# A second channel product in 7x7 block products, its inner weight sums in DRAM, and both channel products in one interleaved stream

## The chip, the cores and the metric

One Trainium2 chip, one core. The time is the device time of one execution in microseconds (us), taken over three to six executions of each kernel; the kernel before is run on the same chip in the same rounds. The profile is one execution under the hardware profiler. Its engines: PE is TensorE's matmuls, PEld its weight loads, DVE is VectorE, ACT ScalarE, POOL GpSimd, SPq the queue in which SyncE issues transfers. SBUF and PSUM are the core's two on-chip memories; the tiles of this program whose names begin with ps_ lie in PSUM, its other tiles in SBUF.

## The reference, cut to what matters

```python
kv  = einsum('bhsd,bhse->bhde', k, v)           # B = 8, H = 8, S = 576, D = 64
out = einsum('bhsd,bhde->bhse', q, kv)
x   = out / sqrt(mean(out**2) + 1e-6) * g_norm  # reshaped to (B, S, 512)
h   = maximum(x.T @ w_tok1, 0) @ w_tok2         # token mixing, 576 -> 256 -> 576
u   = x + h.T
h2  = maximum(u @ w_ch1, 0) @ w_ch2             # channel mixing, 512 -> 1536 -> 512
return u + h2                                   # all in fp32
```

The last two products, the "channel products", take two thirds of the time. They are worked on in nine groups of 512 rows. Group 0 is a special case that runs while weights are still being mixed; the eight groups after it are alike and are called steady groups here.

## The kernel before

A matrix product cut into 2x2 blocks needs eight block products, or seven with extra sums of blocks (Strassen's scheme in Winograd's form). Done at two levels it is 7 x 7 = 49 for 64. The first channel product already works so in the steady groups; the second is done at one level. They follow each other.

```python
SA = {1: 0, 2: 1, 7: 2, 4: 3, 5: 4, 6: 5, 3: 6}      # where a block or a sum of blocks lies
def a_of(o, n):                                       # weight block: outer product o, inner product n
    o, n = SA[o], SA[n]
    if o > 3:
        return late["w2"][:, o - 4, n]
    return w_ch1[:, o, n] if n < 4 else late["w1"][:, o, n - 4]   # all in SBUF
...
def channel1(g):                                      # first product: 7 outer x 7 inner
    padd = lambda o, a, b: tensor_add(o, a, b, engine=nc.gpsimd)   # whole 128x1536 sums on GpSimd
    ...
        def product(n, name, start, stop):            # one block product: 3 matmuls of 128 columns
            for w in range(W):
                matmul(at[name][:, w], lhsT=a_of(o, n)[:, ts(w, P)],
                       rhs=uT[g][:, SB[o], SB[n]], start=(start and w == 0), ...)
    ...
def channel2(g):                                      # second product: 7 products, one level
    def product(n, ps, start, stop):                  # 12 matmuls of 256 columns
        for p in range(2):
            for s in range(NS):
                matmul(ps[:, p], lhsT=V[g][n - 1][:, s, p], rhs=w2_of(n)[:, s], ...)
    ...
for g in range(NG):
    fetch_u(g + 1)
    extra = prepare(g + 1, t_psum)                    # transposes and sums for the next group
    ...
    for step in channel1(g):
        step()
    for n, step in enumerate(channel2(g)):
        step()
        for f in extra[n:n + 1]:
            f()
```

## Time and profile before

| | before |
|---|---|
| time, median of 3 runs | 912.71 us (912.62 to 914.88) |
| span of the profiled run, granted TensorE clock | 909.4 us, 0.976 |
| one steady group | 71.10 us |
| TensorE, VectorE, GpSimd busy in it | 71.09, 40.67, 20.67 us |

### The profile page before, as it was taken

How to read it: one execution, taken by the hardware profiler on the slowest of the kernel's cores; microseconds unless marked ns; L12 is line 12 of the kernel's file. 1: busy time of each engine (PE TensorE's matmuls, PEld its weight loads, DVE VectorE, ACT ScalarE, POOL GpSimd, SP SyncE). 2: the span in 40 equal slices, each digit the busy share in tenths (PEclk: the TensorE clock that was granted, in tenths of full speed). 3: DMA queues.
4: the chain of work that ended last, by engine and by line, in shares of the span. 5: the costliest groups of instructions: out<-in, count | busy, mean ns of one | idle time of the engine just before them, and what ended most of it. 6: DMA issues, size and time to landing. Idle time of an engine off the chain costs nothing.

```text
span 909.4 us, 12630 instructions
## 1 busy us (share of the span) xinstructions
PE 858.0 (94%) x5136; PEld 727.7 (80%) x5136; DVE 561.9 (62%) x928; ACT 245.1 (27%) x588; POOL 168.2 (18%) x62
## 2 busy tenths in 40 slices
PE   5479897997999999999999999999999999999997
PEld 5356454563468889889989989989989989989986
DVE  1677887897765695655646736636636546546552
ACT  2556645655311102302301301311211210310210
POOL 1000000000000006304404503602701700800710
PEclk9789998998999999999999999999999999999999
DMA  9994675833140011002001002002002002001002
GB/s 297 325 316 140 242 236 194 264 110 116 39 146 1 1 47 47 1 29 66 1 24 70 1 1 93 1 1 93 1 1 93 1 1 94 1 1 47 1 1 47
DMA packets 43578, 72.54 MB, mean 80 GB/s; under 512 B 2688, under 2 KB 21120, under 8 KB 43520
## 3 DMA queue, kind: packets, MB, share of 16 engines
q1 hardware_dynamic: 42160, 70.53, 23.6%
q10 hardware_dynamic: 1360, 1.21, 0.4%
q8 instruction: 40, 0.66, 0.3%
q14 instruction: 18, 0.15, 0.1%
HBM read 52.85 MB, written 18.87 MB: 79 GB/s over the span
## 4 chain that ended last, share of the span: by engine, by line
PE 82%; DVE 8%; DMA 4%; ACT 3%; issue 1%; POOL 0%; POOLq 0%; SPq 0%; ACTq 0%; DVEq 0%
PE ps_w L127 34%; PE ps_v L127 32%; PE ps_h L127 5%; PE ps_u L127 5%; DMA v_in<-in_v_dram 2%; ACT x L318 2%; PE ps_ut L411 2%; PE ps_kv L127 2%; PE ps_o L127 1%; DVE x L296 1%; DMA raw<-in_moe_w_tok_dram 1%; DVE part L178 1%; ACT sq L295 1%; PE ps_r L127 1%; DVE uT L118 1%
## 5 line engine op out<-in xcount | busy, mean ns | idle before, releaser
L127 PE MATMUL ps_v<-uT,w 128*128 128x128 f32 (+1 forms) x1656 | 209.6, 280 | 0.1
L127 PEld LDWEIGHTS ps_v<-uT,w 128*128 128x128 f32 x1656 | 198.2, 192 | 2.1 <-DVE uT L118 0.3
L118 POOL TENSOR_TENSOR vs<-vs,v 128x1536 f32<-128x1536 f32 x8 | 27.6, 3445 | 668.3 <-DVE vs L118 668.3
L127 PE MATMUL ps_v<-uT,w_ch 128*128 128x128 f32 (+1 forms) x864 | 124.1, 287 | 0.5 <-DVE u L118 0.5
L127 PEld LDWEIGHTS ps_v<-uT,w_ch 128*128 128x128 f32 x864 | 112.3, 192 | 4.6 <-issue 0.8
L127 PE MATMUL ps_w<-d,vs 128*128 128x256 f32 x432 | 96.8, 380 | 0.5 <-DVE vs L118 0.4
L127 PE MATMUL ps_w<-w_ch,v 128*128 128x256 f32 x432 | 96.2, 379 | 0.0
L127 PE MATMUL ps_w<-w_ch,vs 128*128 128x256 f32 x432 | 96.2, 379 | 0.0
L118 DVE TENSOR_TENSOR vs<-ps_v,u 128x384 f32<-128x384 f32 (+1 forms) x123 | 69.0, 561 | 39.7 <-PE ps_v L127 30.9
L127 PEld LDWEIGHTS ps_w<-d,vs 128*128 128x128 f32 x432 | 80.7, 190 | 12.6 <-issue 1.5
L127 PEld LDWEIGHTS ps_w<-w_ch,vs 128*128 128x128 f32 x432 | 81.5, 190 | 10.7
L127 PEld LDWEIGHTS ps_w<-w_ch,v 128*128 128x128 f32 x432 | 80.8, 190 | 10.3
L124 ACT COPY t<-ps_v 128x384 f32<-128x384 f32 (+1 forms) x59 | 28.5, 484 | 210.3 <-PE ps_v L127 193.5
L318 ACT ACTIVATE x<-x,inv 128x64 f32<-128x64 f32 x288 | 70.9, 337 | 16.9 <-DVE inv L314 16.9
L127 PE MATMUL ps_h<-x,w_tok 128*128 128x512 f32 (+1 forms) x160 | 69.2, 625 | 4.0 <-DVE w_tok L118 4.0
L127 PE MATMUL ps_u<-h,w_tok 128*128 128x512 f32 (+1 forms) x160 | 69.2, 623 | 0.0
L118 DVE TENSOR_TENSOR u<-ps_v,t 128x384 f32<-128x384 f32 (+1 forms) x59 | 33.3, 564 | 48.2 <-PE ps_v L127 46.3
L121 ACT ACTIVATE v<-v 128x1536 f32<-128x1536 f32 (+1 forms) x30 | 39.5, 1316 | 72.6 <-DVE v L118 72.6
L118 POOL TENSOR_TENSOR v<-v,vs 128x1536 f32<-128x1536 f32 x16 | 55.1, 3442 | 19.9 <-DVE vs L118 9.7
L118 DVE TENSOR_TENSOR uT<-uT 128x512 f32<-128x512 f32 (+1 forms) x68 | 56.6, 874 | 2.1 <-ACT uT L124 1.6
L118 DVE TENSOR_TENSOR u<-ps_w,u 128x512 f32<-128x512 f32 x18 | 12.4, 692 | 71.2 <-PE ps_w L127 71.2
L127 PEld LDWEIGHTS ps_h<-x,w_tok 128*128 128x128 f32 (+1 forms) x160 | 27.5, 200 | 35.7 <-issue 33.8
(74 smaller groups left out, 926.3 us busy)
## 6 DMA issues: line engine op xcount, KB each, us to landing
qT<-in_q_dram SPq DMA_DIRECT2D x8, 1152.0 KB, 7.7
xg<-u_dram SPq DMA_DIRECT2D x9, 1024.0 KB, 5.6
k_in<-in_k_dram SPq DMA_DIRECT2D x16, 512.0 KB, 5.6
u_dram<-x SPq DMA_DIRECT2D x16, 512.0 KB, 3.0
out_dram<-xg SPq DMA_DIRECT2D x16, 512.0 KB, 2.8
v_in<-in_v_dram SPq DMA_DIRECT2D x14, 512.0 KB, 6.6
raw<-in_moe_w_ch_dram SPq DMA_DIRECT2D x16, 384.0 KB, 5.7
raw<-in_moe_w_ch_dram SPq DMA_DIRECT2D x12, 512.0 KB, 4.0
```

Of the source, the lines that this page charges most:

```text
L118: keep(engine.tensor_tensor(out=o, in0=a, in1=b, op=op))
L121: keep(nc.scalar.activation(o, a, AF.Relu))
L124: keep(nc.scalar.copy(o, a))
L127: keep(nc.tensor.matmul(*a, **kw))
L178: keep(nc.vector.scalar_tensor_tensor(out=part, in0=lo, scalar=2.0 ** -52, in1=part, op0=ALU.mult, op1=ALU.mult))
L295: keep(nc.scalar.activation(sq, o, AF.Square))
L296: keep(nc.vector.tensor_mul(x3, o, g_sb.to_broadcast([P, n * H, D])))
L318: keep(nc.scalar.activation(x3[:, i], x3[:, i], AF.Copy, scale=inv[:, i]))
L411: keep(nc.tensor.transpose(pt[:, c], xg[g][:, i, ts(c, P)], ident))
```

## The change

Its intent is to do the second product at two levels too. That asks for inner sums of both its operands. Those of the weights (for both products now) are no longer kept in SBUF: they are worked out once, written to DRAM in pieces of 576 KB, and one piece is loaded for each outer product, 14 a group. The two products become one stream: one block product is a "place" of 0.67 us, outer product n starts at place 7n, its seven block products are spread over the places 0, 1, 3, 4, 6, 9 and 12 from there, and so they mix with those of the next outer product. Other engines' work is attached to places by `put`. `b` is the first place of a group's second product. The core of the diff, with comments added:

```diff
+    IN = {1: {5: 0, 6: 1, 3: 2}, 2: {5: 0, 6: 1, 4: 2}}
+    def part(weight, o, n, sums=None):
+        if n in IN[weight]:                      # an inner sum: from the loaded piece
+            t = sums[:, IN[weight][n]]
+            return t if weight == 1 else t.rearrange("p (w e) -> p w e", w=W)
 ...
+    PLACE = {1: 0, 2: 1, 6: 3, 5: 4, 7: 6, 4: 9, 3: 12}
+    def outer(place, size, mul, to, base=None):
+        at(1, "a", True, False, lambda: read(temp("t1", 1), 0, 0))   # bank a is read after
+        at(2, "c", True, True)                                       # each of 1, 6, 7, 4
 ...
+    def fetch_sums(n):
+        if n < len(order):
+            w, _, o = order[n]
+            sums[n] = sums_tile()
+            dma(sums[n], sums_dram[w, o])
 ...
+        put(b + 22, *padd(3, 3, 1))              # in channel1: b is the first product's own
+        put(b + 29, *padd(2, 2, 1))              # first place; GpSimd, two halves each
+        put(b + 36, *padd(1, 4, 3))
+        put(b + 43, *padd(7, 5, 4))
 ...
+        put(b - 8, *ins[1][0], ins[1][1])        # in channel2: inner sums of the left operand,
+        put(b + 1, *halves(make_a21))            # "sv", 4 per outer product, on VectorE
+        put(b + 4, *ins[4][0])
+        put(b + 6, *halves(sum1))
+        put(b + 9, ins[4][1], *halves(sum2))
 ...
+        put(b + 63, xadd(0, 1, 3), do(store, g, xg, 0), do(fetch_x, g + 1))
 ...
-    late["xg"] = pool("xg", 2)
+    late["xg"] = pool("xg", 1)
 ...
+    weave(body, lasts + [f for _, f in inner1] + [f for fs, _ in inner2 for f in fs])
+    fetch_x(1)                                   # the passage from group 0 to the stream
+    for n in range(3):
+        fetch_sums(n)
 ...
-        for step in channel1(g):
-            step()
-        for n, step in enumerate(channel2(g)):
-            step()
+    for place in range(max(beside) + 1):
+        if place in products:
+            products[place]()
+        for step in beside[place]:
+            step()
```

## The prediction

> **What bounds the kernel now.** I read the busy shares first, then the chain that ended last, then the instructions in order of time in one steady group, and last what the SyncEngine's DMA queue waited for.
>
> ```profile
> PE 858.0 (94%) x5136; PEld 727.7 (80%) x5136; DVE 561.9 (62%) x928; ACT 245.1 (27%) x588; POOL 168.2 (18%) x62
> PE 82%; DVE 8%; DMA 4%; ACT 3%; issue 1%; POOL 0%; POOLq 0%; SPq 0%; ACTq 0%; DVEq 0%
> PE ps_w L127 34%; PE ps_v L127 32%; PE ps_h L127 5%; PE ps_u L127 5%; DMA v_in<-in_v_dram 2%; ACT x L318 2%; PE ps_ut L411 2%; PE ps_kv L127 2%; PE ps_o L127 1%; DVE x L296 1%; DMA raw<-in_moe_w_tok_dram 1%; DVE part L178 1%; ACT sq L295 1%; PE ps_r L127 1%; DVE uT L118 1%
> ```
>
> TensorE is busy 94% of the span, and two thirds of the chain is the two channel products: ps_v (the first, already seven block products at two levels, 7x7) and ps_w (the second, at one level). By stage (the table of windows) one steady group, 478.2 to 549.3 us, takes 71.10 us, TensorE busy in 71.09 of them and VectorE in 40.67. There are eight such groups; group 0, with weights mixed at one level, is a separate 75 us stage ahead of them. In the chain of waits a steady group reads:
>
> ```profile
> 407.29 32.83 PE ps_v L127 x294
> 440.11 5.18 PE ps_w L127 x24
> 445.30 0.45 PE ps_ut L411 x4
> 445.75 5.40 PE ps_w L127 x24
> 451.59 5.18 PE ps_w L127 x24
> 457.20 5.18 PE ps_w L127 x24
> 462.82 15.54 PE ps_w L127 x72
> ```
>
> The first product is 32.83 us for 294 records (147 matmuls, two records each: fp32). One block product is 6 records, 0.670 us, so 0.1117 us a record of 128 columns. One second-channel product is 24 records of 256 columns, 5.18 us, 0.2159 us a record. A group is 32.83 + 7 x 5.18 + 4 transposes of 0.43 = 70.8 us: nothing else is on the path.
>
> **What the skill says.** "TensorE: Matmul & The Clock Gate", Back-to-back issue gap, gives an isolated gap of N/2.4 + 2.5 ns, 55.8 ns for 128 columns and about 109 for 256. Two passes' worth would be 111.7 and 218; the trace has 111.7 and 215.9. The fixed part is small, so halving the width costs only 3.4% (2 x 111.7 against 215.9). The same page, Why this matters for your kernels, says that a PE gap over about 3 us sends the clock back to half rate; no steady stretch of this trace has such a gap, so it neither confirms nor refutes that. "VectorE: DVE Perf Modes", The perf-mode tier table, has fp32 tensor_tensor at one element a cycle: 128x512 sums take 0.69 us here and 128x1536 1.75, slope 1.04 ns an element, which agrees. "PSUM — Partial Sum Buffer", Engine vs sequencer instructions, has the queues of the three other engines strictly first in, first out: a sum ahead of a bank's read delays that read. The trace shows VectorE serving them in issue order.
>
> **The change, part by part.**
>
> 1. Second product at two levels. Removed per group: 7 x 5.18 = 36.26 us of TensorE. Added: 49 block products of 3 matmuls, 128x128 by 128 columns, the form of the first product: 49 x 0.670 = 32.83. Saved 3.43 us a group. The 0.27 us a group lost to waits (71.1 against 70.83) may go too. Over eight groups **27 to 29 us on the path**. Two levels do 49/56 of the one-level work (-12.5%), of which the narrower matmuls give back three points.
>
> 2. VectorE work per group. Back to back, independent sums start 0.47 us apart at 384 columns, 0.61 at 512, 0.87 at 768 (each duration less some 0.09); a dependent one some 0.12 later. After: first product 8 reads (where a base is added) and 21 writes of 384: 29 x 0.47 = 13.6. u sums, 4 each of 512, 640 and 256: 2.4 + 2.9 + 1.3. Second product: 21 bank reads of 128 columns, about 0.2 each (estimate from the 0.28 of the 128-column kvp copies), 4.2; inner sums of its left operand, new, 28 of 384, 13.2 and some 1.7 for dependence; a21 and sums s1 to s4 in halves, 10 x 0.87 = 8.7; results into x, 11 x 0.61 = 6.7. Sum **55 us**, against 40.7 before, beside 67.4 of TensorE. Overall VectorE fits (81%), but unevenly: from eight places ahead of the second product to its 38th place, 46 x 0.67 + 1.7 of transposes = 32.5 us of TensorE time, I count 14.8 inner sums, 9.0 halves, 3.6 into x, 4.6 and 4.5 bank reads = 36.5. It overflows by 4 us. A write out of bank b has 4 places (2.7 us) before the next product into that bank; a VectorE read of bank a has 2 (1.3 us). So most of the backlog is swallowed and some reaches TensorE. Walking that stretch place by place by hand I find three waits of 0.8, 0.5 and 1.2 us. I take half that, 1.2 us a group, because my sums err to both sides and the placing looks tuned: **+10 us** over eight groups (0 to 20).
>
> 3. ACT and POOL. ACT gets 20 copies of 0.48, 28 of about 0.26, 12 relus of about 0.5 and 4 turns of 0.58: 26 us a group. POOL does 8 halves for 6 wholes of 3.45: about 14 us for 20.7. Both stay far off the path.
>
> 4. Sums in DRAM. 14 pieces of 3x384 floats on 128 partitions are 590 KB each; every block product loads one, 8.3 MB a group, with x (1.05 MB), the transposition source (1.05) and stores (1.05) 11.4 MB in 67 us, 170 GB/s. The early slices carry 297 to 325 GB/s at 94 to 99% busy, so this is half the DMA. A piece is asked for some 11 places (7.4 us) before its first use; 1 MB lands in 5.6 us, so it is hidden, though where x is fetched just ahead of it on the same queue only barely.
>
> 5. Group 0 and the passage to the stream. In the first product of group 0, VectorE takes 21 more sums (9.9 us) into 16.5 us of idle time; in its second, 28 weight sums replace 28. I expect under 1 us there. The passage is another matter: before, VectorE ends it late, and the queue then waits for the store:
>
> ```profile
> 337.40 0.69 DVE L118 TENSOR_TENSOR xg<-ps_w,xg 128x512 f32<-128x512 f32 x1
> ...
> 331.98 6.52 SPq L115 DMA_DIRECT2D out_dram<-xg  x2
> 341.03 0.37 SPq L115 DMA_DIRECT2D xg<-u_dram  x1
> ```
>
> The last ps_w ends at 334.6, the sum into x at 338.1, and the fetch into the freed buffer is issued at 341.03, landing 6 us later. That fetch was not needed for a whole group, so it cost nothing. After, there is one x buffer, and the first pieces of inner sums are asked for *behind* the fetch of x on the same queue. The stream can do two block products (1.3 us) before the third needs a piece. So: 3.5 us to the sum, 2.9 to the store's end, 0.4 issue, then 1.6 MB at 325 GB/s, 5 us, and some 2 of latency: about 13.5 us from TensorE's last product, of which 1.3 is worked through. **12 us of idle TensorE**, and about 1.5 more (estimate from the skill's half clock) until the clock is back, less 1.4 that this passage (72.5 against 71.1) loses today: **+12 us, once**.
>
> 6. The end. The last block products have nothing interleaved between them, so each waits for its bank; final sums and store are as now: +2 us.
>
> Sum: 912.7 - 29 + 10 + 12 - 1 (waits that may overlap) + 2 = 906.7. As the schedule seems laid out with care I shade the VectorE waits to about 6 us: **903 us**.
>
> **Rivals.**
>
> (a) TensorE stays the only bound, passage hidden: 912.7 - 29 + 2 = 886. For: VectorE at 81%, DMA at half, eleven places of lead. Against: the queue order of the passage, which the trace shows waiting for that very store.
>
> (b) VectorE becomes the bound in the second product: its 36.5 us for 32.5 become waits of 4 us a group and 32 in all, 927. For: strict order and dependent sums. Against: the loose places after the 38th and the bank slack.
>
> (c) DMA binds: pieces land late every time x is fetched, 1 us a group or more, +8 to +16. For: store, wait, 1 MB and piece share one queue; it waited 2.5 us for a store seven times already. Against: half the bandwidth is free.
>
> (d) Narrow matmuls are not as quick in the second product as in the first: at 0.125 us a record nothing would be saved. Against: same form, same type, and 0.1117 holds for hundreds of records on end.
>
> **Range and chances.** The gain is firm at 27 to 29 us. Over 2% (under 894.5) leaves only 9 to 11 us for passage, waits and end together; the passage alone eats that unless I misread it: 0.2. Slower by over 2% (over 931) needs (b) and (c) in full: 0.05. Within 2%: 0.75. For 8 in 10: passage 7 to 15, waits 0 to 16, end 0 to 4 give roughly 891 to 917.
>
> **What would show it.** Step 1: second product in 6-record pieces of 0.67 us, ps_w's TensorE time about 32.8 us a group. Step 2: waits of PE for VectorE in the first 35 places of a second product, VectorE busy about 55 us a group or somewhat more. Step 4: no PE wait for DMA in steady groups, some 170 GB/s. Step 5: a PE gap of 8 to 15 us after group 0, ended by the DMA of sums, with the clock below full after it. Wrong if the period of a steady group is over 70 us (waits) or the passage is under 5 us (the queue does not block as I read it).

## More of the kernel before

The page cuts the span into 40 equal slices of 22.7 us; a digit is the busy share in tenths.

```profile
PE   5479897997999999999999999999999999999997
POOL 1000000000000006304404503602701700800710
PEclk9789998998999999999999999999999999999999
```

The steady groups begin in the fifteenth slice. From there TensorE is at 9 in all slices but the last, and its clock in all: next to nothing in these groups keeps it waiting. GpSimd comes in bursts, one per group. What VectorE does during a burst turned out to matter; the instructions in order of time around one burst, GpSimd first, then VectorE (start, duration, engine, line, output and inputs; in brackets the idle time before it and what ended that):

```profile
417.40 3.44 POOL L118 TENSOR_TENSOR vs<-vs,v 128x1536 f32<-128x1536 f32 x1 [46.49 <-DVE vs L118]
435.02 6.98 POOL L118 TENSOR_TENSOR vs<-vs,vs 128x1536 f32<-128x1536 f32 x2
```

```profile
418.77 0.56 DVE L118 TENSOR_TENSOR u<-ps_v,u 128x384 f32<-128x384 f32 x1
442.04 1.76 DVE L454 SCALAR_TENSOR_TENSOR vs<-vs,v 128x1536 f32<-128x1536 f32 x1 [1.33 <-POOL vs L118]
```

During the burst VectorE runs only sums with one operand in PSUM (ps_v), and they take the 0.56 us that they take elsewhere. Its first sum of two SBUF tiles starts at 442.04, after GpSimd's last sum has ended at 442.00, on whose result it waits. The same holds for every other GpSimd sum of this trace: this kernel never has a VectorE sum of two SBUF operands beside one. I did not see that when I predicted.

## The result, and the profile after

The changed kernel took **980.17 us** (978.59 to 981.5, four runs), the kernel before beside it 912.66. The ratio is 1.073 (95%: 1.071 to 1.076): 7% slower, where I had predicted 1% faster. A ratio here and below is the mean time of one kernel's fast runs over that of the other's in the same rounds, so not quite the ratio of the medians. The result is correct.

The page after:

```profile
PE 861.8 (88%) x6144; PEld 761.1 (78%) x6144; DVE 724.5 (74%) x1384; ACT 331.1 (34%) x924; POOL 122.1 (12%) x78
PE   6478997979999868998998999899899799899896
PEclk9789898989999978999999899899899899999998
```

TensorE's row has a 6 in the fifteenth slice (342.9 to 367.3 us), just behind the stream's first products at 336.6, and dips to 8 or 7 again and again after it; the clock's row dips too. In the page's account of the chain that ended last, VectorE has 28%, where it had 8%.

One steady group before and one after, from the table of windows (start:end and length, then busy time and instructions of PE, PEld, DVE, ACT, POOL, then granted clock, DMA share, GB/s):

```profile
478.20:549.30 71.10, 71.09 (x480) 66.34 (x479) 40.67 (x57) 13.66 (x22) 20.67 (x6) 1.00 0.08 30
```

```profile
457.90:534.20 76.30, 70.35 (x606) 69.33 (x606) 59.33 (x112) 24.45 (x64) 14.95 (x9) 0.98 0.45 151
```

This group takes 76.3 us, the mean over the seven periods from 380.64 to 923.02 us is 77.5. Unhindered it would be 98 products of 0.67 and four transposes of 0.43, 67.4 us. So each steady group is 6.4 us longer than before where it should have been 3.7 shorter.

What TensorE waited for from 336 us on (engine and bank, then what it waited for; us in all, times, longest):

```profile
PE ps_a L127 <- DVE t L118: 30.0, 8, 3.8
PE ps_a L127 <- DMA sums<-sums: 17.8, 6, 14.0
PE ps_a L127 <- DVE uT L118: 7.0, 7, 1.0
PE ps_b L127 <- DVE r L118: 6.9, 8, 1.1
PE ps_a L127 <- DVE v L118: 2.6, 9, 1.1
```

(t and u are what is read out of bank a, r and v results of a second and of a first product and sums of them, uT the transposed left operand of the first product with its sums.) Two entries stand out: one wait of some 3.75 us in each of the eight groups, and one of 14.0 us, once. The same view of the kernel before, from 330 us on, has 0.9 us in all.

**The wait of each group.** VectorE in order of time ahead of it, then GpSimd, then TensorE:

```profile
457.07 0.77 DVE L118 TENSOR_TENSOR sv<-v 128x384 f32<-128x384 f32 x1
457.87 2.05 DVE L118 TENSOR_TENSOR sv<-sv,v 128x384 f32<-128x384 f32 x1
459.95 2.04 DVE L118 TENSOR_TENSOR sv<-v,sv 128x384 f32<-128x384 f32 x1
461.92 0.55 DVE L118 TENSOR_TENSOR sv<-v 128x384 f32<-128x384 f32 x1
462.38 0.54 DVE L118 TENSOR_TENSOR t<-ps_a,v 128x384 f32<-128x384 f32 x1
...
471.83 0.56 DVE L118 TENSOR_TENSOR sv<-sv,v 128x384 f32<-128x384 f32 x1
```

```profile
453.82 7.75 POOL L118 TENSOR_TENSOR v<-v,v 128x768 f32<-128x768 f32 x4 [2.74 <-ACT t L124]
```

```profile
458.40 0.83 PE L127 MATMUL ps_a<-uT,w 128*128 128x128 f32 x6
462.98 1.65 PE L127 MATMUL ps_a<-uT,sums 128*128 128x128 f32 x6 [3.75 <-DVE t L118]
464.43 2.26 PE L127 MATMUL ps_b<-uT,sums 128*128 128x128 f32 x12
466.52 0.83 PE L127 MATMUL ps_a<-uT,w_ch 128*128 128x128 f32 x6
```

The product that ended at 459.2 filled bank a. VectorE has to read it (t<-ps_a) before the next product into bank a, but four sv sums were issued ahead of that read. The second and third took 2.05 and 2.04 us, while such a sum some 14 us later, with GpSimd at rest, takes 0.56. GpSimd's four sums run from 453.82 to 461.57, and the first sv sum after that is back at 0.55. The read came at 462.38 and TensorE went on at 462.98. Then it ran at half speed for most of 3.5 us: one product shown with 1.65 us in place of 0.83, two with 2.26 in place of 1.50 (the last product of a row is shown with its modelled end; in a row they start 0.67 apart).

**The passage**, once, from the instructions in order of time (SPq lines are the issue of transfers):

```profile
339.68 0.68 DVE L118 TENSOR_TENSOR xg<-ps_w,xg 128x512 f32<-128x512 f32 x1
340.38 0.39 SPq L115 DMA_DIRECT2D out_dram<-xg  x1
343.63 0.37 SPq L115 DMA_DIRECT2D xg<-u_dram  x1
344.09 3.60 SPq L115 DMA_DIRECT2D sums<-sums  x3
352.12 1.62 PE L127 MATMUL ps_a<-uT,sums 128*128 128x128 f32 x6 [13.98 <-DMA sums<-sums]
```

This is the order of step 5 of the prediction: the sum into x, the store, the fetch of x that waits for the store, and behind it the pieces that TensorE needs. What each link costs, e3 and e7 show below.

### The profile page after: what moved, and what is told of

Same layout as the page of the kernel before. It is cut to its first block, busy times and chain, and to the rows that moved or that the text cites. A ratio compares the mean times of both kernels' runs of the same rounds, so it can differ in the third digit from the quotient of the medians.

```text
span 979.6 us, 16051 instructions
## 1 busy us (share of the span) xinstructions
PE 861.8 (88%) x6144; PEld 761.1 (78%) x6144; DVE 724.5 (74%) x1384; ACT 331.1 (34%) x924; POOL 122.1 (12%) x78
## 4 chain that ended last, share of the span: by engine, by line
PE 53%; DVE 28%; DMA 9%; issue 4%; ACT 4%; SPq 0%; DVEq 0%; ACTq 0%
PE ps_a L127 19%; PE ps_b L127 10%; DVE v L118 7%; DVE sv L118 7%; PE ps_u L127 5%; PE ps_h L127 5%; PE ps_c L127 4%; DMA sums<-sums 4%; PE ps_v L127 4%; PE ps_w L127 3%; ACT x L351 2%; DVE xg L118 2%; DVE uT L118 2%; DVE r L118 2%; DMA out_dram<-xg 2%
## 5 line engine op out<-in xcount | busy, mean ns | idle before, releaser
L118 POOL TENSOR_TENSOR v<-v,v 128x768 f32<-128x768 f32 x64 | 119.4, 1892 | 803.9 <-DVE v L118 779.0
L124 ACT COPY u<-ps_a 128x384 f32<-128x384 f32 (+1 forms) x192 | 67.9, 354 | 213.0 <-PE ps_a L127 194.7
L118 DVE TENSOR_TENSOR v<-ps_b,u 128x384 f32<-128x384 f32 x112 | 60.5, 552 | 60.8 <-PE ps_b L127 44.1
L127 PE MATMUL ps_a<-uT,sums 128*128 128x128 f32 x336 | 54.5, 304 | 48.1 <-DVE t L118 30.0
L127 PE MATMUL ps_b<-uT,sums 128*128 128x128 f32 x672 | 95.5, 296 | 0.0
L127 PEld LDWEIGHTS ps_b<-uT,sums 128*128 128x128 f32 x672 | 90.3, 212 | 0.0
L127 PE MATMUL ps_a<-uT,w_ch 128*128 128x128 f32 x576 | 83.5, 286 | 7.0 <-DVE uT L118 7.0
L127 PEld LDWEIGHTS ps_a<-uT,w_ch 128*128 128x128 f32 x576 | 76.0, 202 | 8.2 <-issue 8.1
L118 DVE TENSOR_TENSOR uT<-uT 128x512 f32<-128x512 f32 (+3 forms) x96 | 62.6, 663 | 2.7 <-ACT uT L124 1.9
L127 PE MATMUL ps_a<-uT,w 128*128 128x128 f32 x432 | 59.0, 276 | 0.0
L118 DVE TENSOR_TENSOR u<-ps_a,v 128x384 f32<-128x384 f32 x32 | 17.8, 558 | 52.5 <-PE ps_a L127 52.5
L127 PEld LDWEIGHTS ps_kv<-v_in,k_in 128*128 128x128 f32 x320 | 40.1, 203 | 14.8 <-DMA v_in<-in_v_dram 6.3
```

The costliest lines, as they stand in the source:

```text
L118: keep(engine.tensor_tensor(out=o, in0=a, in1=b, op=op))
L124: keep(nc.scalar.copy(o, a))
L127: keep(nc.tensor.matmul(*a, **kw))
```

## The experiments

Eleven kernels ran. Two theories compete for the wait of each group. **Exclusion**: a VectorE sum of two SBUF operands and a GpSimd sum that reads SBUF hold each other up. The Trainium skill, "SBUF — State Buffer", section Who interferes with whom, states it: VectorE's second SBUF input comes through a read interface that it shares with GpSimd, and the shared pair is an exclusive lock. The prediction does not use it. The rival (V) is that **VectorE is simply too full** there, as rival (b) of the prediction had it, and its long sums are a symptom. All times beside a ratio are medians.

### e1_sv_late: the four sums moved past GpSimd's burst

```diff
-        put(b - 8, *ins[1][0], ins[1][1])
-        put(b + 1, *halves(make_a21))
+        put(b - 1, *ins[1][0][:2])
+        put(b + 2, ins[1][0][2], ins[1][1])
+        put(b + 3, *halves(make_a21))
```

> One group of sums of the second product's first left operand is issued seven to ten places later, when GpSimd has finished its four adds. Theory P (GpSimd and VectorE exclude each other: a VectorE sum with both operands in SBUF waits for the GpSimd add in flight): no sum of sv takes over 0.8 us any more (two of each group took 2.05), the 3.75 us wait of PE for DVE t goes under 0.5, the half-clock stretch after it goes too, a steady group takes 71 to 73 us instead of 76 to 79, and the time is 935 to 945. Theory V (VectorE has simply too many sums; GpSimd has no part in it): the wait moves to the place where the sums went, the group stays over 74.5, the time over 960. This run cannot tell P from a mere bad placing; e2_pool_write does.

Measured: 948.87 us, ratio 1.041 (1.039 to 1.042), correct. All sv sums take 0.55 to 0.56 us, GpSimd's sums 1.82 where they took 1.89, and the wait for t is gone from the list. But the groups take 72.6 to 76.2 us, 73.8 on average, more than expected, as the same work now delays something else:

```profile
PE ps_a L127 <- DMA sums<-sums: 19.5, 5, 13.5
```

The waits for r (results read out of bank b) come to 14.8 us in 16, double the 6.9 us of the changed kernel. This moves 31 us, but changes two things, the collision and the order, so it does not tell the theories apart.

### e2_pool_write: GpSimd writes without reading (wrong results on purpose)

```diff
-            return halves(lambda i: tensor_add(*(half(v_tile(g, t), i) for t in (o, x, y)),
-                                               engine=nc.gpsimd))
+            return halves(lambda i: keep(nc.gpsimd.memset(half(v_tile(g, o), i), 0.0)))
```

> Wrong results on purpose: the GpSimd adds are replaced by writes of zero to the same tiles at the same places, so GpSimd reads nothing; the VectorE stream is the changed kernel's, instruction for instruction. Theory P (contention for SBUF reads): all sv sums take 0.55 to 0.6 us, back to back at 0.47 to 0.59; the PE wait for DVE t shrinks from 3.75 to 0.5 to 1.2 us (four sums still stand ahead of the read), PE keeps its full clock, a steady group takes 71.5 to 73.5. Theory V (VectorE's own load): the sums stay at 2.05 us or the wait at over 3 us, the group at 76 to 79. If P holds but the contention is for any SBUF use by GpSimd, writes too, some sums would still be long, by the length of a GpSimd write.

VectorE's orders are untouched. Measured: 937.08 us, ratio 1.028 (1.026 to 1.029). The groups of instructions (count | busy us, mean ns | idle before) and then TensorE's wait:

```profile
L713 POOL MEMSET v<- 128x768 f32 x64 | 44.5, 738 | 831.5 <-DVE v L118 831.5
L118 DVE TENSOR_TENSOR sv<-sv,v 128x384 f32<-128x384 f32 x56 | 31.2, 558 | 1.9
```

```profile
PE ps_a L127 <- DVE t L118: 4.5, 8, 0.6
```

The mean of these sums was 771 ns in the changed kernel and is 558. The wait falls from 3.75 to 0.56 us, the group from 77.5 to 72.2 on average (71.4 to 73.9). The order alone is worth 0.56 us; my walk by hand had 0.8 for it. But GpSimd's timing changes too: a write takes 0.74 us for 1.89, and the last write of each group ends 5.1 us or more before the sv sums begin. So no sum ran beside a write. The run shows the same VectorE order with GpSimd at rest; whether a GpSimd write alone would hold a sum up, which was the last point of the expectation, it does not show, and no other run does. That VectorE's own load is not the cause, the next run tests harder.

### e6_adds_on_vector: GpSimd's sums put on VectorE

```diff
-                                               engine=nc.gpsimd))
+                                               engine=nc.vector))
```

> The changed kernel with the eight adds of a group moved from GpSimd to VectorE, at the same places, results right. Theory P (exclusion between the two engines): no sv sum over 0.6 us although VectorE has 7 us more of work a group; the PE wait for DVE t shrinks from 3.75 to 0.5 to 2.5 us; the group takes 72 to 76 us, the time 935 to 965, under the changed kernel's 980. Theory V (VectorE's own load makes the wait): more load, more waiting, 985 to 1010 us.

This gives VectorE 64 more sums of 0.95 us, 61 us of work. If VectorE is too full, it gets worse. Measured: 947.86 us, ratio 1.040 (1.038 to 1.042), correct: 32 us *faster* than the changed kernel. VectorE's busy time rose not by 61 us but by 26.5, from 724.5 to 751.0: most of the rest had been blocked time shown as busy (e1, without the collision, shows 699.0). The sv sums are at 553 to 558 ns and the waits for t at 4.8 us for eight. The rival falls as the cause of the 3.75 us. What it is right about comes up again below: with the added work a wait of 7.3 us for u appears.

### e3_passage and e7_order_only: the passage

```diff
# e3_passage
-    weave(body, lasts + [f for _, f in inner1] + [f for fs, _ in inner2 for f in fs])
-    fetch_x(1)
+    weave(body[:11], lasts + [f for _, f in inner1] + [f for fs, _ in inner2 for f in fs])
+    body[11]()
     for n in range(3):
         fetch_sums(n)
+    body[12]()
+    fetch_x(1)
# e7_order_only: only these two exchanged
-    fetch_x(1)
     for n in range(3):
         fetch_sums(n)
+    fetch_x(1)
```

> Only the passage from group 0 to the stream is changed: the weight sums are finished a little earlier, and the three first pieces of sums are asked for ahead of the last store of x and of the fetch of x, not behind them. If the 14 us gap of PE comes from the order in the one DMA queue (sum into x, store, fetch of x, then the pieces): the gap goes to 1 to 6 us, the time falls by 9 to 14 us to 966 to 971, and the steady groups stay at 76 to 79 us. If the gap comes from VectorE being late with the u sums or from the DMA engines being full, the gap stays over 10 us and the time over 975.

> Only the order of two requests in the one DMA queue at the passage: the three first pieces of sums ahead of the fetch of x, everything else as changed, VectorE's order too. In the trace the pieces are asked for at 344.1, behind a 3.2 us store that the fetch of x waits for, and the first lands at 352.1. If the order is the cause, the first piece is asked for at about 342 and lands 4 to 5 us later: the PE gap goes from 14.0 to 7 to 10 us and the time down by 4 to 7, to 973 to 976. If the DMA engines' load is the cause, gap and time stay within 2 us.

Measured: e3 967.27 us (ratio 1.061, 1.059 to 1.064), e7 974.53 (1.069, 1.066 to 1.071), both correct. The first product that waits for a piece, in e3 and then in e7:

```profile
340.09 0.91 PE L127 MATMUL ps_a<-uT,sums 128*128 128x128 f32 x6 [3.77 <-DMA sums<-sums]
```

```profile
349.95 1.62 PE L127 MATMUL ps_a<-uT,sums 128*128 128x128 f32 x6 [10.87 <-DMA sums<-sums]
```

The steady groups are as they were (30.0 us for t in both). The fetch of x ahead of the pieces costs 3.1 us of the 14; 7.1 more go when VectorE's weight sums are also finished earlier and the pieces asked for ahead of the last store (e3 does both at once, so it does not part them); 3.8 remain. For the order of the queue alone I had expected a gap of 7 to 10 us; it was 10.9.

### e8_x_late: the fetch of x moved behind the pieces, on top of e1

```diff
# with the edit of e1
-        put(b + 63, xadd(0, 1, 3), do(store, g, xg, 0), do(fetch_x, g + 1))
+        put(b + 63, xadd(0, 1, 3), do(store, g, xg, 0))
+        put(b + 70, do(fetch_x, g + 1))
```

> e1_sv_late with the steady fetch of x seven places later, behind the piece of sums of that place. In e1_sv_late PE waits 1.8 to 2.1 us for a piece in four of the groups, right after the store and the fetch of x. If the fetch's wait for the store, in the same queue, delays the piece: these waits vanish, the group falls from 74.5 to 72.0 to 72.7, the time from 948.9 to 935 to 943. If the pieces are late because the DMA engines are busy, the waits stay and the time is within 3 us of 948.9.

Measured: 941.97 us, ratio 1.033 (1.032 to 1.035), correct, 7 us less than e1. The waits for pieces within the groups are gone; what is left is the passage:

```profile
PE ps_a L127 <- DMA sums<-sums: 14.3, 1, 14.3
```

So rival (c) is true in small: a fetch that waits for a store blocks the pieces behind it on the queue. It costs a microsecond a group, not bandwidth.

### e4_all and e5_tuned: everything at once

e4 joined e1, e3 and e8 with three small moves, of which one was an error of mine: an inner sum moved ahead of a reader of the block that it overwrites.

```diff
# e4_all, beside the edits of e1, e3, e8
-        put(b + 17, ins[6][1], *ins[5][0])
+        put(b + 14, ins[6][1])                   # wrong: sum4 at b + 15 still reads that block
+        put(b + 17, *ins[5][0])
-        put(b + 28, *ins[2][0], ins[2][1])
+        put(b + 29, *ins[2][0], ins[2][1])
-        put(b + 52, xadd(1, 0, 7), xadd(1, 1, 7))
+        put(b + 58, xadd(1, 0, 7), xadd(1, 1, 7))
# e5_tuned: without the wrong move, and instead
-        put(b + 6, *halves(sum1))
+        put(b + 8, *halves(sum1))
-        put(b + 33, *ins[3][0], ins[3][1])
+        put(b + 36, *ins[3][0], ins[3][1])
```

> The two edits above, the fetch of x seven places later and behind the piece of that place, and three small moves of VectorE work (one sum, four sums, two additions into x) away from the reads that PE waits for. If the waits found in the trace are all there is: a steady group takes 67.5 to 70 us, the passage 2 to 6, and the time is 895 to 912, level with or up to 2% under the kernel before. If removing one wait only exposes the next (VectorE at 59 us a group is too full), groups stay at 71 to 74 us and the time at 920 to 940.

> e4_all with its error mended (one sum ran ahead of a reader of the block that it overwrites; it is back in its place) and two more moves: sums s1 two places later, behind the write out of bank b that PE waits for, and the last outer product's left sums three places later. e4_all's steady group was 70.45 us, of which some 3 us are lost at three places, the largest (1.1 us) in front of the product behind that write. If waits are what is left: correct, a steady group of 68.5 to 70, 898 to 912 us in all, level with the kernel before or up to 1.5% under it. If VectorE at 55.7 us a group cannot be placed any better, the group stays at 70 to 71.5 and the time at 912 to 922.

Measured: e4 917.69 us with a wrong result (relative error 0.31), so its time counts for nothing but the hint that it leaves. e5 914.32 us, ratio 1.002 (1.001 to 1.004), correct, a group 70.1 us: the second case of the expectation. The largest wait is now 10.9 us in 16 for VectorE's v, at most 1.5 us each.

### e9_best, e10_best_collide: the cost of the collision by itself

e9 smooths the passage further, puts the first sums of the left operand at b - 2 and issues the halves of two other VectorE sums in the order in which they are read. e10 is e9 with one line put back, so that the four sums fall on GpSimd's burst again.

```diff
# e9_best, beside e8's late fetch and e5's later ins[2], ins[3] and xadd
+        put(b - 2, *ins[1][0][:2])
+        put(b + 2, ins[1][0][2], ins[1][1])
+        put(b + 3, *halves(make_a21))
+        put(b + 6, do(sum1, 0))
+        put(b + 8, do(sum2, 0), do(sum1, 1))
+        put(b + 9, ins[4][1], do(sum2, 1))
+    weave(body[:11], fill[:-3] + [do(fetch_sums, 0)] + fill[-3:])   # and e3's order of the rest
# e10_best_collide, against e9
-        put(b - 2, *ins[1][0][:2])
-        put(b + 2, ins[1][0][2], ins[1][1])
+        put(b - 8, *ins[1][0], ins[1][1])
```

> e5_tuned with the two waits that its trace still has taken on: the sums s1 and s2 are made half by half in the order in which the outer products read them (PE lost 1.3 us a group in front of one), the two first sums of the group that collided with GpSimd go one place earlier, just behind GpSimd's last add (0.4 us lost), and the first piece of sums is asked for one piece earlier at the passage. If these waits are all: a steady group of 67.6 to 68.8 us instead of 70.1, a passage gap of 1 to 3.5 us without loss of clock, 893 to 904 us in all, 1 to 2% under the kernel before. If each cured wait exposes another of the same size, 908 to 915.

> e9_best with one thing undone: the four sums of the first left operand back at the place of the changed kernel, beside GpSimd's adds. Theory P: two sums of each group are 2.05 us long again, PE waits 3.5 to 4 us for DVE t and runs at half clock behind it, 5 to 6 us a group, so 40 to 48 us above e9_best. If the collision only mattered because the rest of the schedule was full as well, less than 20 us.

Measured: e9 912.42 us, ratio 1.000 (0.998 to 1.003), five of seven groups 69.7 us and two 71.4; e10 948.01 us, ratio 1.039 (1.037 to 1.041); both correct. The longest waits of e9 and then of e10:

```profile
PE ps_a L127 <- DVE v L118: 13.0, 9, 1.6
```

```profile
PE ps_a L127 <- DVE t L118: 30.0, 8, 3.8
PE ps_a L127 <- DVE v L118: 9.9, 9, 1.6
```

The one line costs 35.6 us, 4.5 a group, somewhat under what I had expected and well above the rival's figure. It brings back the same 30.0 us of waits for t. By e2, some 0.56 us a group of it would be there without the collision, from the order alone. e9 is not quite free of the collision either: at b - 2 the first sv sum of each group still meets the end of GpSimd's last one and takes 0.95 to 0.98 us for 0.55. All of TensorE's waits in the stream add up to 44.2 us in e10 and 15.9 in e9 (smaller ones of at most 0.5 us each, and those for pieces, 3.9 us in e10 and 2.0 in e9, are not shown), so 28.3 us are waits; most of the rest goes to the slower clock, which stood at 0.50 for 30.7 us of e10's stream and 6.8 of e9's. One gap at the passage (3.27 us for a piece, 1.33 in e9) and the slow clock behind it, some 3.6 us of the profiled difference, are not the collision's: both kernels have the same order there.

### e11_one_sum: the last large wait

In e9 the second outer product's seventh block product waits for the inner sum ins[4][1]. e11 issues it earlier.

```diff
-        put(b + 6, do(sum1, 0))
+        put(b + 6, do(sum1, 0), ins[4][1])
-        put(b + 9, ins[4][1], do(sum2, 1))
+        put(b + 9, do(sum2, 1))
```

> e9_best with one VectorE sum of 0.55 us moved ahead of 1.8 us of others: the seventh left operand of the second outer product, behind which PE lost 2.0 us in every group of e9_best (wait for DVE v, 1.56 us at the latest product's modelled end). If the loss is the order in VectorE's queue: the wait goes to under 0.3 us, the group from 69.7 to 67.5 to 68.5 us, the time to 896 to 904, 1 to 2% under the kernel before. If VectorE is too full in this stretch for any order: the wait moves to the next product and the group stays above 69.2, the time above 907.

Measured: 911.87 us, ratio 0.999 (0.997 to 1.001), correct, the group again at 69.7 us. The wait has moved, to r and (4.2 us in 8) to v out of another bank:

```profile
PE ps_b L127 <- DVE r L118: 5.7, 8, 1.1
```

So here the rival is right in its second place: from about b - 8 to b + 38 VectorE is nearly full, busy 30.97 of 33.40 us in e11 (439.1 to 472.5), and in the orders that I tried each wait cured shows another. That no order would do is not shown. No version beat the kernel before by more than the noise.

## Why the prediction was wrong

**Step 1, the matmuls: right.** A product of the second kind is 6 records, 0.67 us apart, as assumed; TensorE's own work is 67.4 us a group for 71.1, and the 27 to 29 us of gain are in the trace. Rival (d) is out.

**Step 2, VectorE's waits: the step that failed.** "I take half that, 1.2 us a group [...] **+10 us** over eight groups", shaded to 6. Measured: 30.0 + 7.0 + 6.9 + 2.6 = 46.5 us of waits, and on top the clock. Of the three waits walked by hand (0.8, 0.5, 1.2 us), those of the order alone came out near: 0.56 with the collision taken away (e2), 0.83 to 1.1 for r. The load was near too: 59.3 us a group for the predicted 55, and some 56 in e9 with little blocked time in it. What is missing from the step is a mechanism. I priced "inner sums of its left operand, new, 28 of 384, 13.2" at the isolated duration of such sums. In the kernel before every VectorE sum beside GpSimd had an operand in PSUM, so its trace held no case of the price that applies: 2.05 us for 0.56. The page that I should have drawn on for a row with two SBUF inputs and GpSimd at work was "SBUF — State Buffer"; the prediction cites others. Three of the four new b - 8 sums fall into GpSimd's sums. e2 (GpSimd at rest by then, wait 0.56) and e6 (no GpSimd, more work on VectorE, faster) show it, e10 measures it: 35.6 us, of which some 4.5 (8 times 0.56) are the order alone and, in the profiled run, some 3.6 the passage.

The collision costs more than VectorE loses. The two sums lose 1.49 and 1.48 us and the first 0.2, in all 3.2 us; TensorE waits 3.75, as the read of bank a stands behind them; and then it runs slower.

**Step 3, ACT and POOL: right on load, wrong on "far off the path".** 24.5 us for ACT and 14.95 for POOL in the group shown, 26 and 14 predicted. But POOL's sums are what VectorE stood behind: an engine with little to do can be on the path by what it shares.

**The clock.** In step 5 I had counted 1.5 us for a return to half clock, once. "TensorE: Matmul & The Clock Gate", section What's actually happening, has the array fall to half clock after an idle window of about 3.4 us and come back after one busy window. The table of windows gives the granted clock (the number before DMA share and GB/s); two stretches, of the changed kernel behind the gap shown above and of e9:

```profile
462.98:464.43 1.45, 1.45 (x7) 1.45 (x7) 0.88 (x2) 0.00 (x0) 0.00 (x0) 0.50 0.00 0
```

```profile
450.60:454.01 3.41, 3.41 (x18) 3.41 (x18) 3.31 (x7) 0.53 (x2) 0.00 (x0) 0.50 0.23 95
```

In the changed kernel the clock falls to 0.50 in or just behind each of the eight gaps of 3.72 to 3.75 us and stays there for 3.41 us (twice) or 6.83 us (six times): one or two windows of the page's length, so the lengths agree. Behind the gap shown above, three products took 3.54 us, from 462.98 to 466.52, and not 2.01. In all eight, TensorE worked for 39.0 us at half clock, which costs half of that, 19.5 us, or 1.5 to 2.9 at a time. So the clock is a term of every group. In this kernel nothing slow follows the waits of 0.8 to 1.5 us. But a gap of 3.4 us is not needed: the clock fell 2.0 us into the first of the eight gaps (which began at 382.04; it fell at 384.08), and in e9, whose longest wait is 1.56 us, it fell behind two of the eight waits of that length. What decides which ones is not shown. The passage's slow products add 2.3 us (the four from 352.12 took 4.97 us and not 2.68).

**Step 4, DMA: right on bandwidth, wrong on "hidden".** 149 to 155 GB/s in two groups for the predicted 170. (The "94 to 99% busy" of the early slices is a misreading: the trace gives the first three a DMA share of 0.97 to 1.09. Nothing rests on it.) But 17.8 - 14.0 = 3.8 us of waits for pieces in the groups, by the order of the queue (e8). "Only barely" was the right reading of the risk.

**Step 5, the passage: right.** Predicted 12 us with the clock, by the chain that the trace shows; measured 13.98 of gap and 2.3 of clock. The fetch of x itself is 3.1 of the 14 (e7); VectorE's late sums and the last store ahead of the request make 7.1 (e3). TensorE enters the stream at 336.64 where it was 334.62, 2 us where I had said under 1.

**Step 6, the end: near.** From the end of the last product it is 7.8 us, before it was 6.0.

The terms, from the two profiled runs:

| term | predicted | measured |
|---|---|---|
| TensorE's own work | -27 to -29 | 8 x (67.4 - 71.1) = -29.6 |
| waits for VectorE (and 0.4 for ACT) | +6 to +10 | +46.9 |
| waits for DMA in the groups | 0 | +3.8 |
| half clock in the groups | 0 | 39.0 / 2 = +19.5 |
| passage, its clock, the later entry | +12 | 14.0 + 2.3 + 2.0 = +18.3 |
| end | +2 | +1.8 |
| sum | -6 (with -1 for overlap), shaded to -10 | +60.7 of the +70.2 between the spans |

About 9.5 us are not in a term. Some 6.2 of them are an artefact of how waits are counted: from the modelled end of the product before, 0.83 us after its start, where the next in a row starts after 0.67, so 0.16 us in each of 39 waits. The rest is not assigned.

**Rivals.** (a) assumed the passage hidden; it is not. (b) had the size nearest of all, 4 us a group and 927, but for the load of VectorE and not for the exclusion; its load is real, as e11 suggests, and costs at most some 2 us a group (69.7 for 67.4). (c) is there with half a microsecond a group.

**Where the gain is in e9.** Five of its seven full groups are 1.4 us shorter than before; two are not, 71.4 us, as the clock fell in them. So the seven save 6.3 us. The stream from first to last product takes 564.0 us and before 568.8, 4.8 less: the last group has less to mix with and takes more. It starts 0.5 us later and ends 3.5 us later after its last product (9.5 for 6.0), so 0.8 us are left. Which order of VectorE's work would bring the group to 67.4 stays open, and so does whether the last group could be shortened.

## What to carry to other kernels

Before new VectorE sums of two SBUF tiles are placed, look at what GpSimd does in the same microseconds: the duration of such a sum in a trace where GpSimd was at rest, or where the other operand was in PSUM, is not its price. Where VectorE, which here worked its sums off in the order of issue, also frees PSUM banks, look for a delay in three places: the sum's own, the wait of the product behind the read, and the slower clock after the gap, which here followed eight of eight gaps of 3.75 us in the changed kernel and six of eight in e10. When a cure moves work in a nearly full stretch, look for the wait that it makes in the next place, and price the whole group's period, not the wait that is gone.

## What the Trainium skill lacked or had wrong

- "SBUF — State Buffer", Who interferes with whom, was right that such sums contend: two sums of 384 columns took 2.05 and 2.04 us for 0.56 beside GpSimd sums. It names two slow-downs (VectorE 6.8 times, GpSimd 1.5 times) without the operations. Here VectorE lost some 1.5 us at a time, about what was left of a GpSimd sum, and GpSimd 0.3: the two sums of a group that were met took 2.11 to 2.13 us, the others 1.80 to 1.82. That a GpSimd write alone does not contend, no run here shows.
- "VectorE: DVE Perf Modes", The perf-mode tier table, gives durations for fp32 sums of SBUF tiles without a word on GpSimd; the shared interface comes up only in a later section, Two Vector instructions with no wait between them. Here such a sum took 3.7 times its usual duration (2.05 for 0.56 us). Who prices from the table alone gets it wrong, as I did.
- "TensorE: Matmul & The Clock Gate", What's actually happening, puts the fall to half clock after an idle window of about 3.4 us. Here it also came behind two of eight waits of 1.56 us (e9, granted clock 0.50 from 450.60 to 454.01 and from 522.28 to 525.69), so a shorter gap can be enough. And a gap just over the window need not cost anything: e10 has eight gaps of 3.73 to 3.75 us. Two of them were followed by no slow product at all (products shown with 0.94, 1.50 for two, and 0.83 us), the others by up to four slow ones (1.65, 2.77 for two, 1.41). The cost of one such gap lay between about 0.1 and 2.6 us, and the page gives no such range.
- "TensorE: Matmul & The Clock Gate", Back-to-back issue gap, gives N/2.4 + 2.5 ns for an isolated matmul, 55.8 ns for 128 columns, and does not say that fp32 takes a multiple of it. Here three fp32 matmuls of 128 columns take 0.670 us in a long row, 223 ns each, four times the page's figure. That factor stands in "FP8 and Floating Point Precision", TensorE Precision Notes (four passes for true fp32), and agrees.
